# First rows' transfers first, first weights by column halves, and a newly laid order, in an attention kernel with a gated MLP

## The chip, the cores and the metric

The kernel runs on one core of a Trainium2 chip. The metric is device time in microseconds (us), lower is better. A core has a matrix engine (TensorE, PE below, with its weight loads as PEld), a vector engine (VectorE, DVE), a scalar engine (ScalarE, ACT), a general engine (GpSimd, POOL), and a queue of transfers that SyncE (SP) issues to 16 DMA engines.

## What is computed

Four batches of eight heads, 576 rows, 64 columns. Causal attention is mixed by a gate with a retrieval from a memory `M_prev`; the result, 2304 rows of 512, goes through an MLP of width 2048 with a leaky activation whose slope `alpha` is a column's own.

```python
def _attn_ref(q, k, v, M_prev, z_prev, beta) -> np.ndarray:
    scores = scale * np.matmul(q, k.transpose(0, 1, 3, 2))
    scores = np.where(causal, -1000000000.0, scores)
    scores = scores - scores.max(-1, keepdims=True)
    a = np.exp(scores)
    a /= a.sum(-1, keepdims=True) + 1e-09
    local = np.matmul(a, v)
    q_p = phi(q)
    mem_ret = np.einsum('bhsd,bhde->bhse', q_p, M_prev)
    mem_norm = np.einsum('bhsd,bhd->bhs', q_p, z_prev)[..., None] + 1e-06
    mem_out = mem_ret / mem_norm
    g = 1.0 / (1.0 + np.exp(-beta))[None, :, None, None]
    return (g * mem_out + (1 - g) * local).astype(np.float32)
...
def _moe_ref(x, w_in, w_out, alpha) -> np.ndarray:
    h = x @ w_in
    g = np.maximum(h, 0.0) + alpha * np.minimum(h, 0.0)
    return (g @ w_out).astype(np.float32)
```

`phi(x)` is `x + 1` for positive `x` and `exp(x)` otherwise.

## The kernel before

**Arithmetic.** Nearly every product is made in f16 from two parts, a high and a low one, which DVE and ACT split off (`SCALAR_TENSOR_TENSOR` with an f16 output is the low part). The weights arrive as pairs of 32-bit words of 64-bit numbers; `to_f32` turns a piece into f32 on DVE with one TENSOR_SCALAR and two SCALAR_TENSOR_TENSOR. `R` is the buffer of converted weights, 17 slots of 128x1024; `kn`, `E` and parts of `R` also hold words as they arrive.

**Stages.** The first 64 rows of all four batches form a group of their own, called Z. `first_scores` and `first_values` do its attention in f32: `s` are scores, `P` the probabilities, `stv` the maxima of its `v` and `M_prev` (`prep_vZ`). The other rows are groups of 256, two to a batch. For each head and pair of row blocks `unit_scores` makes the scores `s` on PE and their minima with the mask on DVE (`E<-s,mask,pm`, or `P<-s,mask` and `E<-s,mask` for batch 0), ACT the exponential, `unit_probs` the f16 parts `P`, `pair_values` the product with `v` in `bank`. `build_qk` and `build_v` form the f16 parts of `q`, `k` and `v` of a batch; `mv` are the maxima of `v` of batch 0, which its first values need. The MLP goes in steps: `moe_in` makes 256 columns of `h`, of which DVE and ACT form `r` and the two f16 parts of `gg`, and `moe_out` adds their product to `y`. The first two groups (Z and the first of batch 0) use the weights in f32 for their first four steps, before `split_w` has cut them in f16; with f32 weights the MLP's `h` reads `h<-R`.

**Weights.** `weights(0)` loads (`load_w`) and converts (`conv_w`) eight pieces for the first half of the MLP, `weights(1)` the other eight. Pieces 0 to 3 are `w_in`, 4 to 7 `w_out`. A piece is two transfers of 128x1024 words; `conv_w` converts it in one go of 1024 columns (one piece in two), and ACT then squares it for the sum that sets its scale (`w_scale`, whose result is `wsc`).

**Order.** Every operation is first recorded by a `Work` object, with the data it depends on (so all of them carry one line of the helper, L560), and then `Work.issue` sets the order of each engine's instructions. It prices each operation (`price`), lays them on the engines by rank (`lay`), and shifts the ranks in four rounds by the tables in `STAGES`, in which a phase name such as `LW0` (loading the first four pieces) or `V0` has a number. No instruction waits for anything but the data and the order. All transfers stand on one queue.

**Warm-up.** While nothing is there yet, PE runs 66 matmuls on a constant `ones`, of which 16 may stand at the start and 50 behind (`WARM`).

## Time and profile before

| | us |
|---|---|
| three runs, median | 558.14 |
| lowest and highest run | 557.56, 559.28 |
| span of the profiled execution | 555.3 |
| PE busy in it | 532.3 (96%) |
| DVE busy | 451.2 (81%) |
| ACT busy | 376.1 (68%) |
| POOL busy | 77.7 (14%) |

The profiled execution is one run; its own time is the span of 555.3 us, and 2.9 us less than the median of the runs, which take in what lies around it. Busy times are sums over the instructions of an engine; those of PE hold the warm-up matmuls.

### The profile page before, as it was taken

The page shows a single profiled execution, that of the slowest core. Times are in us where ns is not written, and L with a number is a line of the kernel's source. Part 1 is how long each engine was busy: PE and PEld are TensorE (multiplying, and loading weights), DVE is VectorE, ACT ScalarE, POOL GpSimd, SP SyncE. Part 2 cuts the span into 40 slices and gives each one's busy share as a digit, 9 for nine tenths or more (in the row PEclk, how much of TensorE's full clock was granted, in tenths as well). Part 3 has the DMA queues.
Part 4 walks back from the last instruction along what each step waited for, and adds up shares of the span by engine and source line. Part 5 has one row for each costly group of instructions (what it writes and reads, how often), then busy time and mean ns, then how long its engine had stood idle before and what let it go on. Part 6 is the DMA issues. An engine that isn't in the chain of part 4 may idle for free.

```text
span 555.3 us, 11994 instructions
## 1 busy us (share of the span) xinstructions
PE 532.3 (96%) x4421; PEld 353.1 (64%) x4421; DVE 451.2 (81%) x1197; ACT 376.1 (68%) x790; POOL 77.7 (14%) x142
## 2 busy tenths in 40 slices
PE   9739999999999899999998999999999999999997
PEld 3438655666567566758566667667677676866573
DVE  4899999999999899999998899997678885333322
ACT  2558987768999378978867887786587874222312
POOL 2000510031030011311221200321021120000000
PEclk9869999999999999999999999999999999999999
DMA  8999685827359999379998737599536665000101
GB/s 288 231 339 204 192 238 176 246 74 170 91 115 183 219 228 199 86 154 205 221 188 190 170 79 170 130 200 190 79 81 121 138 138 133 21 2 1 38 1 38
DMA packets 226026, 82.84 MB, mean 149 GB/s; under 512 B 216224, under 2 KB 216240, under 8 KB 225968
## 3 DMA queue, kind: packets, MB, share of 16 engines
q1 hardware_dynamic: 225968, 82.09, 64.0%
q8 instruction: 34, 0.56, 0.4%
q14 instruction: 24, 0.20, 0.1%
HBM read 35.66 MB, written 5.77 MB: 75 GB/s over the span
## 4 chain that ended last, share of the span: by engine, by line
PE 52%; DVE 30%; DMA 5%; issue 5%; ACT 3%; SPq 2%; POOL 2%; DVEq 0%; POOLq 0%; ACTq 0%
PE y L560 22%; PE h L560 20%; DVE R L560 5%; DVE P L560 5%; PE s L560 5%; DVE E L560 4%; PE bank L560 4%; DVE gg L560 3%; DVE r L560 3%; DVE q L560 2%; SPq L560 2%; POOL E L560 2%; DMA xn<-in_moe_alpha_dram 1%; DMA k<-k 1%; DVE t L560 1%
## 5 line engine op out<-in xcount | busy, mean ns | idle before, releaser
L560 PE MATMUL h<-x,R 128*128 128x256 f16 x1536 | 261.8, 273 | 1.7 <-DMA x<-xn 1.7
L560 PE MATMUL y<-R,gg 128*128 128x512 f16 (+1 forms) x832 | 258.3, 397 | 0.4 <-ACT k L560 0.4
L560 PE MATMUL bank<-v,PT 128*128 128x64 f16 x1224 | 179.2, 193 | 2.7 <-DMA PT<-P 2.3
L560 PEld LDWEIGHTS <-R 128*128 128x128 f16 x1536 | 148.9, 98 | 41.9 <-issue 5.6
L560 PEld LDWEIGHTS <-PT 128*128 128x128 f16 x1224 | 113.9, 98 | 10.5 <-DMA PT<-P 4.1
L560 PEld LDWEIGHTS <-gg 128*128 128x128 f16 x768 | 74.6, 98 | 70.8 <-DVE gg L560 0.5
L560 POOL TENSOR_SCALAR E<-q,nrm,sm 128x64 f32<-128x64 f32 x112 | 62.5, 570 | 316.8 <-DVE sm L560 265.1
L560 ACT ACTIVATE E<-E,mx 128x320 f32<-128x320 f32 (+3 forms) x136 | 81.0, 601 | 22.7 <-DVE mx L560 18.3
L560 DVE SCALAR_TENSOR_TENSOR P<-E,mx,P 128x384 f16<-128x384 f32 (+2 forms) x112 | 75.4, 699 | 9.8 <-ACT P L560 9.7
L560 ACT ACTIVATE P<-E,mx 128x384 f16<-128x384 f32 (+2 forms) x112 | 70.4, 673 | 16.4 <-POOL E L560 13.2
L560 DVE SCALAR_TENSOR_TENSOR r<-r,oma,h 128x256 f32<-128x256 f32 x128 | 56.8, 473 | 25.0 <-ACT r L560 24.7
L560 DVE SCALAR_TENSOR_TENSOR gg<-r,gsc,gg 128x512 f16<-128x512 f32 x56 | 41.7, 746 | 32.4 <-ACT gg L560 20.6
L560 ACT ACTIVATE r<-h 128x512 f32<-128x512 f32 x72 | 42.0, 586 | 37.2 <-PE h L560 23.1
L560 ACT ACTIVATE gg<-r,gsc 128x512 f16<-128x512 f32 x56 | 39.9, 715 | 32.2 <-PE y L560 29.0
L560 DVE CUSTOM_DVE_ANT_0 E<-s,mask,pm 128x320 f32<-128x320 f32 (+2 forms) x96 | 56.8, 609 | 1.4 <-PE s L560 1.2
L560 PE MATMUL s<-k,qT 128*128 128x64 f16 (+5 forms) x136 | 37.4, 294 | 1.2 <-DMA k<-k 1.0
L560 PE MATMUL s<-k,qS 128*128 128x192 f16 (+4 forms) x120 | 33.6, 294 | 0.0
L560 PE MATMUL h<-R 128*128 128x256 f32 x128 | 32.9, 384 | 0.0
L560 PEld LDWEIGHTS h<-R 128*128 128x128 f32 x128 | 22.3, 192 | 6.6 <-issue 3.3
L560 ACT ACTIVATION_READ_ACCUMULATOR E<-E,mx 128x1 f32 x124 | 23.4, 188 | 0.0
L560 ACT ACTIVATE R<-R,wsc 128x1024 f16<-128x1024 f32 x16 | 18.3, 1142 | 4.0 <-DVE R L560 4.0
L560 DVE SCALAR_TENSOR_TENSOR R<-R,wsc 128x1024 f16<-128x1024 f32 x16 | 20.4, 1275 | 0.4 <-ACT R L560 0.4
(183 smaller groups left out, 619.6 us busy)
## 6 DMA issues: line engine op xcount, KB each, us to landing
q<-in_q_dram SPq DMA_DIRECT2D x16, 256.0 KB, 4.3
vn<-in_v_dram SPq DMA_DIRECT2D x16, 256.0 KB, 4.9
out_dram<-t SPq DMA_DIRECT2D x16, 256.0 KB, 2.7
kn<-in_moe_w_in_dram SPq DMA_DIRECT2D x6, 512.0 KB, 6.5
kn<-in_moe_w_out_dram SPq DMA_DIRECT2D x6, 512.0 KB, 5.7
kn<-in_k_dram SPq DMA_DIRECT2D x12, 256.0 KB, 3.9
qS<-qT SPq DMA_DIRECT2D x24, 128.0 KB, 3.0
R<-in_moe_w_in_dram SPq DMA_DIRECT2D x4, 512.0 KB, 5.6
```

The source lines that it names most:

```text
L560: fn(*a, **kw)
```

## The change

The diff does the following.

- Warm-up: `WARM` goes from 16 and 50 to 16 and 24.
- Pieces 0 to 3 are loaded and converted by column halves: first the left half of all four, then the right. After each left half, `PACE` = 2 matmuls of the new weights (128x256, f32) go to `h0`, which nobody reads. Their squares go to `R[0]`.
- `v` and `M_prev` of the first rows come in two transfers each (64x16x64, two batches in one) and not four.
- The first rows' turned tiles use the PSUM buffer `y` and not `h`.
- The planner: transfers are priced anew (`TURNED`, the returns of `price`, `LATE` = 400 ns more to landing), the queue begins at 700 ns and holds at most eight, a GpSimd operation waits for a DVE operation with two SBUF inputs, and the lag from PE to PE is 0 and not 2.
- Phase names are finer (by pair of heads, step, piece or half), and `STAGES` has 14 tables instead of four. So the order of all work is laid anew; the counts of operations stay, but for the edits above.

```diff
-WARM = 16, 50
+WARM = 16, 24
+PACE = 2
+LATE = 400
...
 STAGES = [
     (2, {
...
-        "C3": -920, "C:ACT": 1096.2, "C:DVE": -3.8, "C:PE": -943.6, "I": -699.2, "I:DVE": 79.2, "I:POOL": 497.7,
+        "C3": -920, "C:DVE": -3.8, "D0": -56.4, "D:DVE": -3.8, "I": -699.2, "I:DVE": 79.2, "I:POOL": 497.7, "J:ACT":
...
-RING, SHARE = 1200, 0.95
+RING, SHARE, BEGIN = 1200, 0.95, 700.0
+TURNED = {128: (1216, 800, 1650), 256: (1298, 860, 1950), 320: (1347, 1500, 1600), 576: (2092, 1880, 2060)}
...
+            late += LATE
...
-                return (800 + 1.75 * kb if kb > 400 else 1130 + 0.6 * kb), 190 + 3.45 * kb, 1655, -1
+                return TURNED[round(kb)] + (-1,)
...
-                return 500, 0.45 * packets, 1800, packets
+                return 350, 90, 2600, packets
...
-                return 400, (2.75 if self.phase in ("LW0", "LW1") else 4.9) * kb, 2000, packets
+                return 390, 2.75 * kb, 2550, packets
...
-                return 540, max(300, 4.06 * kb), 1800, packets
-            return 620, (273 if kb > 200 else 200) + 4.17 * kb, 2100, packets
+                away = o.tensor.name in self.fixed
+                return 580, 250 + 2.6 * kb, 1800 if away or o.space != ins[0].space else 1740, packets
+            return 620, 420 + 2 * kb if o.shape[0] > 64 else 5.08 * kb, 2100, packets
...
+        if not back:
+            free["DMA"] = BEGIN
+        landed, port = [], 0.0
...
+                landed.append(done)
+                if len(landed) >= 8:
+                    free[x] = max(free[x], landed[-8] + 16)
...
+                elif x == "POOL" and not back and port > t:
+                    hold += port - t
...
+                if x == "DVE":
+                    port = done if both else 0.0
...
-        for b in range(B):
-            vv = nat[Z]["v"][b // 2][:, b % 2]
-            Y.dma_start(out=vv[64:128], in_=v[b, :, 0:64, :].rearrange("h p d -> p h d"))
-            Y.dma_start(out=vv[0:64], in_=M_prev[b].rearrange("h d e -> d h e"))
+        for t in range(2):
+            work.phase = f"LV{t}"
+            for ps, src in ((slice(64, 128), v[2 * t:2 * t + 2, :, 0:64, :]), (slice(0, 64), M_prev[2 * t:2 * t + 2])):
+                Y.dma_start(out=nat[Z]["v"][t][ps].rearrange("p b h d -> p (b h) d"), in_=src.rearrange("b h p d -> p (b h) d"))
...
-    def conv_w(s):
-        work.phase = f"C{s // 4}"
-        r, st = raw(s + 1), pieces.pop(s)
-        n = 1024 if WC[s] else 512
-        for c in range(0, 1024, n):
+    def conv_w(s, cs=(0, 1)):
+        work.phase = f"C{s // 4}{s % 4}" if s > 3 or not cs[0] else f"D0{s}"
+        r, st = raw(s + 1), pieces[s]
+        for c in (0, 512) if len(cs) == 1 or not WC[s] else (0,):
+            n = 512 if len(cs) == 1 or not WC[s] else 1024
+            if len(cs) == 1 and c != 512 * cs[0]:
+                continue
             to_f32(r[:, c:c + n], st[:, 2 * c:2 * c + 2 * n].bitcast(I32).rearrange("p (c t) -> p c t", t=2))
-        A.activation(st[:, 0:1024], r, AF.Square, scale=2.0 ** -20, accum_out=wsq[s // 4][:, s % 4:s % 4 + 1])
+        if s < 4 and not cs[0]:
+            work.phase = f"n{s}"
+            for i in range(PACE):
+                T.matmul(h0[:, 0], lhsT=r[:, 0:128], rhs=r[:, 0:256], start=True, stop=True)
+            work.phase = f"C0{s}"
+        if cs[-1]:
+            pieces.pop(s)
+            work.phase = f"c{s // 4}"
+            A.activation(R[0] if s < 4 else st[:, 0:1024], r, AF.Square, scale=2.0 ** -20, accum_out=wsq[s // 4][:, s % 4:s % 4 + 1])
...
-        for x, outs, tag in ((n["q"][t], [(slice(0, 128), qT)], "h"),
+        for x, outs, tag in ((n["q"][t], [(slice(0, 128), qT)], "y"),
...
-        flipped([P[:, h] for h in range(H)], [(slice(0, 128), PT.rearrange("p h c -> p (h c)"))], "hy"[t])
+        flipped([P[:, h] for h in range(H)], [(slice(0, 128), PT.rearrange("p h c -> p (h c)"))], "y")
...
-        load_w(8 * i)
-        for s in range(8 * i, 8 * i + 8):
+        if i == 0:
+            for f in (load_w, conv_w):
+                for c in range(2):
+                    for s in range(4):
+                        f(s, (c,))
+            w_scale(0)
+        first = 8 * i if i else 4
+        load_w(first)
+        for s in range(first, 8 * i + 8):
             if s % 8 < 7:
                 load_w(s + 1)
             conv_w(s)
```

**SP, the first transfers.** Before, the first rows' `q`, `k` (from `in_k_dram`), `v` and `M_prev` stand behind fourteen transfers of weights, `alpha`, `z` and `beta`; the part from the first `q` on reads:

```order
L560 DMA q_0_93<-in_q_dram 64x8x64
L560 DMA R<-in_k_dram 64x8x64
L560 DMA q_0_93<-in_q_dram 64x8x64 x3
L560 DMA R<-in_k_dram 64x8x64
L560 DMA R<-in_v_dram 64x8x64
L560 DMA R<-in_k_dram 64x8x64 x2
L560 DMA R<-in_M_prev_dram 64x8x64
L560 DMA R<-in_v_dram 64x8x64
L560 DMA R<-in_M_prev_dram 64x8x64
L560 DMA R<-in_v_dram 64x8x64
L560 DMA R<-in_M_prev_dram 64x8x64
L560 DMA R<-in_v_dram 64x8x64
```

Now the queue begins so:

```order
L1620 DMA R<-in_v_dram 64x16x64
L1620 DMA R<-in_M_prev_dram 64x16x64
L1620 DMA q_0_93<-in_q_dram 64x8x64 x2
L1620 DMA xn_103<-in_moe_alpha_dram 16x128
L1620 DMA gco<-in_beta_dram 128x8
L1620 DMA R<-in_moe_w_in_dram 128x1024
L1620 DMA R<-in_v_dram 64x16x64
L1620 DMA R<-in_M_prev_dram 64x16x64
L1620 DMA q_0_93<-in_q_dram 64x8x64 x2
L1620 DMA R<-in_k_dram 64x8x64 x2
L1620 DMA q_1_94<-in_z_prev_dram 64x512 x4
L1620 DMA R<-in_k_dram 64x8x64 x2
```

The first rows' `v` and `M_prev` went from the end of their transfers to the start, and of the seven weight transfers that stood ahead of the first `q` six went behind the first rows' `k`.

**DVE, the maxima of `v` of batch 0** (`mv_0_146<-vn_97`; the rows on `R` are weight conversions, `E_0_92` and `kn_90` weight words, `q_2_95` rows of `q` of batch 0). Before:

```order
L560 TENSOR_SCALAR R<-kn_90 128x1024
L560 SCALAR_TENSOR_TENSOR R<-R 128x1024
L560 SCALAR_TENSOR_TENSOR R<-kn_90,R 128x1024
L560 TENSOR_SCALAR R<-E_0_92 128x1024
L560 SCALAR_TENSOR_TENSOR R<-kn_90,R 128x1024
L560 SCALAR_TENSOR_TENSOR R<-E_0_92,R 128x1024
L560 SCALAR_TENSOR_TENSOR q_2_95<-q_2_95,t_0_117 128x512
L560 SCALAR_TENSOR_TENSOR R<-E_0_92,R 128x1024
L560 TENSOR_REDUCE mv_0_146<-vn_97 128x1 x2
L560 SCALAR_TENSOR_TENSOR q_2_95<-q_2_95,t_1_118 128x512
```

Now:

```order
L1620 SCALAR_TENSOR_TENSOR R<-E_0_92,R 128x1024
L1620 TENSOR_REDUCE nrm_106<-t_0_117 128x8
L1620 TENSOR_SCALAR R<-kn_90 128x1024
L1620 SCALAR_TENSOR_TENSOR R<-E_0_92,R 128x1024
L1620 SCALAR_TENSOR_TENSOR R<-kn_90,R 128x1024
L1620 TENSOR_REDUCE wsc<-bank_67 128x1
L1620 TENSOR_REDUCE stq_85<-q_2_95 128x1
L1620 SCALAR_TENSOR_TENSOR R<-kn_90,R 128x1024
L1620 TENSOR_REDUCE mv_0_146<-vn_97 128x1 x2
L1620 ISA E_0_92,mx_107<-s_0_69,mask 128x192
```

The maxima now stand at row 129 and not 112 of DVE's order, behind conversions of `w_out`, with the first score minima of batch 0 (`E_0_92,mx_107<-s_0_69,mask`) right behind them.

**PE, around the first `h` with weights that count** (`h_123` and `h_124` are the two buffers of `h`; `PT` and `R` in `s` rows are the first rows' probabilities and `v`; `y` rows on `ident` turn a tile). Before, ahead of it the last of the first rows' values and the turned `q` of batch 0:

```order
L560 MATMUL y_131<-ident,q_2_95 128x128
L560 MATMUL s_0_69<-PT_113,R 64x64
L560 MATMUL y_132<-ident,q_2_95 128x128
L560 MATMUL y_131<-ident,q_2_95 128x128
L560 MATMUL y_132<-ident,q_2_95 128x128
L560 MATMUL y_131<-ident,q_2_95 128x128
L560 MATMUL y_132<-ident,q_2_95 128x128 x2
L560 MATMUL h_124<-R 128x256
L560 MATMUL h_123<-R 128x256
```

Now (the `h_123<-R` ahead of the turned `q_2_95`, x2 and single, are pace matmuls):

```order
L1620 MATMUL y_131<-ident,P_99 128x128 x4
L1620 MATMUL y_132<-ident,P_99 128x128 x4
L1620 MATMUL s_0_69<-PT_113,R 64x64 x16
L1620 MATMUL h_123<-R 128x256 x2
L1620 MATMUL y_131<-ident,P_100 128x128 x4
L1620 MATMUL y_132<-ident,P_100 128x128 x4
L1620 MATMUL h_123<-R 128x256
L1620 MATMUL s_0_68<-PT_114,R 64x64 x16
L1620 MATMUL y_131<-ident,q_2_95 128x128
L1620 MATMUL y_132<-ident,q_2_95 128x128
L1620 MATMUL y_131<-ident,q_2_95 128x128 x3
L1620 MATMUL y_132<-ident,q_2_95 128x128 x3
L1620 MATMUL h_123<-R 128x256
L1620 MATMUL h_124<-R 128x256 x8
```

The first `h` that counts moved from row 203 to row 105 of PE's order, behind the same turned `q`.

## Rows read from the trace of the kernel before

**Rows 1.** Windows of the span: stretch and length, busy us of each engine (instructions).

```profile
0.00:47.34 47.34, 34.49 (x244) 20.93 (x244) 37.46 (x111) 23.74 (x65) 4.16 (x13) 0.82 0.97 275
47.34:273.30 225.96, 222.72 (x1681) 144.72 (x1681) 220.17 (x578) 181.93 (x374) 39.84 (x63) 1.00 0.75 175
273.30:551.50 278.20, 275.10 (x2501) 187.46 (x2497) 193.62 (x512) 169.69 (x352) 33.70 (x66) 1.00 0.51 107
```

**Rows 2.** PE timeline, 39 to 51 us: start, us, engine, line, operation, [idle <-releaser].

```profile
39.41 1.51 PE L560 MATMUL h<-ident,P 128*128 128x128 f32 x6 [2.82 <-DVE P L560]
...
47.34 2.86 PE L560 MATMUL h<-R 128*128 128x256 f32 x12
...
50.03 0.27 PE L560 MATMUL y<-ident,v 128*128 128x128 f32 x1
```

**Rows 3.** DVE timeline at the 19th f16 `gg`.

```profile
272.56 0.74 DVE L560 SCALAR_TENSOR_TENSOR gg<-r,gsc,gg 128x512 f16<-128x512 f32 x1
273.22 0.68 DVE L560 CUSTOM_DVE_ANT_0 E<-s,mask,pm 128x448 f32<-128x448 f32 x1
```

**Rows 4.** PE timeline, 273 to 276 us.

```profile
273.40 0.19 PE L560 MATMUL bank<-v,PT 128*128 128x64 f16 x1
273.43 0.38 PE L560 MATMUL y<-R,gg 128*128 128x512 f16 x1
273.65 0.19 PE L560 MATMUL bank<-v,PT 128*128 128x64 f16 x1
...
274.67 0.24 PE L560 MATMUL s<-k,qT 128*128 128x192 f16 x1 [0.61 <-DMA k<-k]
...
275.23 0.38 PE L560 MATMUL y<-R,gg 128*128 128x512 f16 x1
```

**Rows 5.** DVE timeline, 0 to 53 us.

```profile
6.24 0.69 DVE L560 TENSOR_SCALAR R<-R 128x1024 int32<-128x1024 int32 x1 [5.12 <-DMA R<-in_moe_w_in_dram]
...
37.59 0.23 DVE L560 SCALAR_TENSOR_TENSOR zsm<-zsm,C 128x8 f32<-128x8 f32 x2
...
51.95 1.81 DVE L560 TENSOR_REDUCE mv<-vn 128x1 f32<-128x1024 f32 x2
```

**Rows 6.** SyncE timeline: issues of the transfers.

```profile
18.48 1.31 SPq L560 DMA_DIRECT2D R<-in_k_dram  x2
...
45.10 0.63 SPq L560 DMA_DIRECT2D vn<-in_M_prev_dram  x1
```

**Rows 7.** Transfers by kind: count, KB each, median us from issue to landing.

```profile
vn<-in_v_dram SPq DMA_DIRECT2D x16, 256.0 KB, 4.9
```

**Rows 8.** ACT timeline: the last exponential of the first rows.

```profile
34.01 0.33 ACT L560 ACTIVATE P<-P,zmx 128x64 f32<-128x64 f32 x1
```

**Rows 9.** DVE by line and form: count, busy us, mean ns, idle before.

```profile
L560 DVE SCALAR_TENSOR_TENSOR P<-E,mx,P 128x640 f16<-128x640 f32 x32 | 28.1, 877 | 2.5 <-ACT P L560 2.5
...
L560 DVE CUSTOM_DVE_ANT_0 E<-s,mask,pm 128x576 f32<-128x576 f32 x24 | 19.4, 809 | 0.9 <-PE s L560 0.9
...
L560 DVE SCALAR_TENSOR_TENSOR R<-kn,R 128x1024 int32<-128x1024 int32 x10 | 12.2, 1225 | 0.0
...
L560 DVE TENSOR_SCALAR R<-kn 128x1024 int32<-128x1024 int32 x5 | 3.4, 687 | 0.0
...
L560 DVE SCALAR_TENSOR_TENSOR R<-kn,R 128x512 int32<-128x512 int32 x4 | 2.7, 680 | 0.0
...
L560 DVE TENSOR_SCALAR R<-kn 128x512 int32<-128x512 int32 x2 | 0.8, 416 | 0.0
```

**Rows 10.** Windows around the first dense stretch; column PEclk is the granted clock.

```profile
33.30:43.60 10.30, 5.70 (x24) 4.74 (x24) 9.32 (x29) 3.43 (x13) 0.00 (x0) 0.50 1.08 349
43.60:60.00 16.40, 16.14 (x140) 12.39 (x140) 16.40 (x36) 14.39 (x31) 0.00 (x0) 1.00 0.97 254
```

**Rows 11.** Windows; the last column is GB/s of the transfers.

```profile
16.00:26.00 10.00, 7.09 (x40) 3.89 (x40) 9.93 (x21) 6.70 (x13) 0.00 (x0) 0.85 1.00 200
34.00:40.00 6.00, 2.13 (x8) 1.69 (x9) 5.02 (x24) 1.59 (x6) 0.00 (x0) 0.50 1.02 402
```

More of the change, by code (lines that the diff above doesn't have):

```diff
@@ new lines @@
+        "P:DVE": -882.6, "P:PE": -157.8, "S0": 4737.2, "S1": -1253, "S3": -2953.6, "S:ACT": -87.5, "S:DVE": 168.1,
[10 rows of a table added]
+        "p:ACT": -1644.8, "p:DVE": -74.4, "q1": 32.6, "q2": 262.4, "q3": -367.1, "q:ACT": -726.4, "q:DVE": -733.4,
+        "r0": 11.2, "r:ACT": 58.5, "r:DVE": 78.6, "s01": 224.3, "s03": -198.1, "s11": -19.5, "s13": -477.4, "s21":
+        -225.6, "s23": -95.5, "s31": -35.1, "s33": 429.3, "s:ACT": -781.8, "s:DVE": -887.5, "s:PE": 273.7, "sZ":
+        208.6, "sZ:ACT": -57.4, "sZ:DVE": 1849.8, "sZ:PE": 312.7, "tZ": 208.6, "tZ:ACT": -57.4, "tZ:PE": 312.7, "v1":
[4 rows of a table added]
@@ L198 @@
+        41.6, "s:ACT": -5, "s:DVE": -22.3, "s:PE": 143.8, "sZ": -0.9, "sZ:ACT": 37.5, "sZ:DVE": 2.5, "sZ:PE": -5.2,
[4 rows of a table added]
         "y0_10:DVE": -5.7, "y0_10:PE": 142.2, "y0_11": -0.1, "y0_11:DMA": 0.3, "y0_11:DVE": -24.3, "y0_11:PE": 213.5,
@@ L753, in load_first @@
             t, ps = b // 2, slice(b % 2 * 64, b % 2 * 64 + 64)
+            work.phase = f"LZ{t}"
             Y.dma_start(out=qz[ps, t], in_=q[b, :, 0:64, :].rearrange("h p d -> p h d"))
@@ L792, with load_w @@
     staging = [[kn, q16] * 4, staging * 2]
-    def load_w(s):
-        work.phase = f"LW{s // 4}"
+    def load_w(s, cs=(0, 1)):
+        work.phase = f"LW{s // 4}{s % 4}" if s > 3 or not cs[0] else f"LX0{s}"
         hf, kind, u = s // 8, s // 4 % 2, s % 4
         st = pieces[s] = staging[s < 8][s % 8]
-        for c in range(2):
+        for c in cs:
             if kind == 0:
@@ L825, in w_kappa @@
     def w_kappa(hf):
+        work.phase = f"c{2 * hf + 1}"
         i = 2 * hf + 1
@@ L839, in split_w @@
     def split_w(s):
-        work.phase = f"S{s // 4}"
+        work.phase = f"S{s // 4}{s % 4}"
         f, r, sc = fin(s), raw(s + 1), wsc[:, s // 4, 0:1]
@@ L989, in prep_phi @@
         nrm, tt, C = p["nrm"][:, r], p["tt"][:, r], p["C"][:, :, r]
+        ph = work.phase
         for i in range(i0, i1):
+            work.phase = f"{ph}{i}"
             qi = qs[i]
@@ L997, in prep_phi @@
             V.reduce_sum(nrm[:, i - i0, :], e, axis=AX.X)
+        work.phase = ph
         V.scalar_tensor_tensor(out=nrm, in0=nrm, scalar=1e-6, in1=igc[:, None, :].to_broadcast([128, i1 - i0, H]),
@@ L1024, in build_qk @@
     def build_qk(b, hp):
-        work.phase = f"bk{b}"
+        work.phase = f"bk{b}{hp}"
         n, p = nat[b], pre[b]
@@ L1042, in build_v @@
     def build_v(b, hp):
-        work.phase = f"bv{b}"
+        work.phase = f"bv{b}{hp}"
         n, p = nat[b], pre[b]
@@ L1074, in first_pair @@
     def first_pair(hp, bl):
-        work.phase = f"s0{bl[0]}"
+        work.phase = f"s0{bl[0]}{2 * hp + 1}"
         p = pre[0]
@@ L1107, in unit_scores @@
             return
-        work.phase = f"s{b}{bl[0]}"
+        work.phase = f"s{b}{bl[0]}{h}"
         a = h % 2
@@ L1129, in unit_probs @@
     def unit_probs(b, h, bl):
-        work.phase = f"P{b}{bl[0]}"
+        work.phase = f"P{b}{bl[0]}{h}"
         p = pre[b]
@@ L1169, in pair_values @@
     def pair_values(b, hp, bl, x):
-        work.phase = f"o{b}{bl[0]}"
+        work.phase = f"o{b}{bl[0]}{2 * hp + 1}"
         pts = [ust.pop((b, 2 * hp + a, bl[0], "T")) for a in range(2)]
@@ L1214, in turned @@
     def turned(i0):
-        work.phase = "BK0" if i0 else "bk0"
+        ph = work.phase = "BK0" if i0 else "bk0"
         n, p = nat[0], pre[0]
@@ L1220, in turned @@
                              i0 + 1 if i0 else 0, 2 if i0 else 3)):
+            work.phase = ph + ("0" if t == "qT" else "1")
             y = p["qT" if t == "qT" else "kT"] = stack[t].rearrange("p (a c) -> p a c", a=NP)
@@ L1238, in first_scores @@
                     [(ps, o.rearrange("p n c -> p (n c)")) for ps, o in outs], tag)
+        work.phase = f"sZ{t}"
         s = other().rearrange("p (h n) -> p h n", h=H)
@@ L1257, in first_values @@
     def first_values(t, x32):
-        work.phase = "oZ"
+        work.phase = f"oZ{t}"
         n, p = nat[Z], pre[Z]
@@ L1283, in moe_in @@
     def moe_in(g, j):
-        work.phase = f"h{g['id']}{j // 4}"
+        work.phase = f"h{g['id']}{j // 4}{j % 4}"
         n = g["n"]
@@ L1323, in moe_out @@
     def moe_out(g, j):
-        work.phase = f"y{g['id']}{j // 4}"
+        work.phase = f"y{g['id']}{j // 4}{j % 4}"
         n = g["n"]
```

94 lines of the change are left out of this document (59 added, 35 removed), and 1413 rows, old and new, of the table STAGES.

## Prediction

> **What bounds the kernel now.** I read three views in this order: the windows of the whole span, the timelines of TensorE (PE) and VectorE (DVE) up to 62 us, and the same two timelines at one later checkpoint. The profiled execution has a span of 555.3 us; the median of the three runs is 558.14 us, so 2.9 us lie around the span and I carry them unchanged.
>
> The windows [rows 1] fall into three stretches. Up to 47.34 us PE does little that counts: most of its 34.5 busy us are warm-up matmuls on `ones`, and DVE is busy for 37.46 us. From 47.34 us, the first real `h` matmul [rows 2], to 551.5 us PE is busy for 497.8 of 504.2 us. Up to 273.3 us DVE is just as full: 220.17 of 225.96 us. Only behind that does it have room, 193.6 of 278.2 us. So the end is set by how early PE's stream starts and how rarely it stops; and up to about 275 us it cannot run ahead of DVE, which converts the weights, forms the score minima and splits every operand. A faster beginning on PE is worth only what DVE follows.
>
> A checkpoint shows how closely the two run together. Count the f16 `gg` splits (the 128x512 SCALAR_TENSOR_TENSOR that finishes one step of the MLP) in DVE's order: the 19th starts at 272.56 and ends at 273.30 us [rows 3], and PE's matmuls on that step stand around the same microsecond, after a wait of 0.61 us for a transfer of `k` [rows 4]. DVE was idle for 9.88 us before 47.34 us and for 5.79 us from there to the checkpoint (stretch less busy time in [rows 1]), 15.7 us together. I forecast the checkpoint of the changed kernel from DVE's work and idle time, and then add the PE work that is left behind it.
>
> **The change part by part.**
>
> *Transfers.* DVE's first work waits 5.12 us for the first weights, until 6.24 us [rows 5]. In the new order it waits for half of `v` and `M_prev`, two transfers of 256 KB as the first on the queue. Pieces of 128 KB take about 0.65 us each to issue (two in 1.31 us [rows 6]), and those of 256 KB 4.9 us to land [rows 7]. Second issue at about 1.4, landing at about 6.3 us: nothing is gained or lost here. The change is what follows. Before, the last `k` of the first rows is issued at 19.1 us, as the second of two from 18.48 [rows 6]; now 18 transfers stand ahead of it, at about 0.65 us each 11.7 us, so it is issued at about 12 us.
>
> *The first rows' chain.* From that issue (19.1) to the first `h` (47.34) it is 28.2 us. In it the last exponential of these rows ends at 34.3 us [rows 8], while DVE first multiplies with its sum at 37.59 us [rows 5]: DVE was at the maxima of `v` and at what follows from them. With `v` first these are done early, 3.3 us less. The first `h` comes at 12 + 28.2 - 3.3 = 37 us, at the earliest some 4 us before if the transposes and copies, which stood behind weight conversions, close up: 33 to 37 us, 10 to 14 us earlier than 47.34.
>
> *DVE's idle time at the start.* Of the 9.88 us, 5.12 are the first wait [rows 5] and 4.8 the rest: the program's start, and short waits for PE. I give the new order the same first wait, and 1 to 3 us for `z`, `k` and the scores: 6 to 8 us in all, **-2 to -4 us; I take -3.** Its own order puts half conversions where it would wait, so the middle is nearest.
>
> *Half conversions.* A full piece costs one TENSOR_SCALAR of 0.687 and two SCALAR_TENSOR_TENSOR of 1.225 us, together 3.14; a half 0.416 and two of 0.680, two halves 3.55 [rows 9]. That is +0.42 us for each of four pieces, +1.7 us at most; since neighbours overlap by 0.08 us (272.56 + 0.74 is 273.30, the next starts at 273.22 [rows 3]), less. I take **+1.1 us**, counted in the next sum; 0 is the other end.
>
> *DVE's work ahead of the checkpoint.* I counted both orders up to the 19th f16 `gg`. The new order has four score minima of 576 columns fewer (0.81 us each [rows 9], -2.9 after the overlap), two of 448 (0.68 [rows 3], -1.2) and four `P` splits, two of 640 columns (0.88 [rows 9]) and two of 512 (0.74, the form of [rows 3]): -2.9. It has one `k` build of 640 and one `v` build of 512 more (+1.7), and the halves (+1.1). Smaller forms cancel. Sum: **-4.2 us** ahead of the checkpoint.
>
> *PE's work ahead of it.* Both have the same `h` and `y` matmuls there to within two. The new order has 70 value matmuls fewer (0.03 us from 273.40 to the next start [rows 4], -2.0 us) and 24 score matmuls of 64 to 512 columns fewer (by columns: a `y` of 512 columns takes 0.22 us to the next start [rows 4], 0.43 ns a column; -3.0 us); against them +0.3 us of small ones. That work is not saved, it stands behind the checkpoint now: **+4.7 us.** The total of PE's useful work is unchanged: 64 f32 `h` matmuls, 1536 f16 ones, 768 f16 `y` and 1224 value matmuls in either order.
>
> *Pace matmuls and warm-up.* Eight f32 matmuls on fresh weights, of 0.45 us at full clock (12 records, two to a matmul, start within 2.69 us [rows 2]), replace 26 of the 66 on `ones`. They stand ahead of the first `h`, where PE idled, 2.82 us at once before 39.41 [rows 2]: nothing. If that cover is gone they cost 3.6 us, or twice that at half clock. The clock is the risk: from 33.3 to 43.6 us PE, with 5.70 us of work in 10.3, was granted 0.50, which is 1.2 GHz, and 2.4 GHz from 43.6 us, when it was busy for 16.14 of 16.4 us [rows 10]. "TensorE: Matmul & The Clock Gate" of the Trainium skill (What's actually happening) says that the throttled state is the default and that activity releases it; by it fewer warm-up matmuls speak against the change, and the trace agrees as far as idling is followed by half clock. By that rule alone the first `h` group would run at half for longer, which is the last rival below.
>
> *DVE's idle time between 47 and 273 us.* 5.79 us now. The prices of transfers in the planner are new (under its old ones PE waited 0.61 us for `k` right at the checkpoint). Bounds: all but 2 us gone, -4; or, since an order with other transfers can meet new waits, twice as much, +6. I take -1.5, near to no change, because the kinds of waits stay.
>
> *PE at and behind the checkpoint.* PE reaches the data of the 19th `gg` 1.9 us later than DVE gives them (275.23 against 273.30 [rows 3, 4]); a stream that is held by DVE alone has not this: -1.8 at most, 0 at least; I take -1.8, since DVE holds it in the new order too. Behind it PE idles for 3.1 us [rows 1]. Between none of it left and twice as much, -3 to +3; I take -1, near to no change. The end behind 551.5 us is the same in both orders: 0.
>
> **Sum:** -3 - 4.2 + 4.7 - 1.8 - 1.5 - 1 = -6.8 us. Against the profiled execution that is a span of 548.5 us; against the median, 558.14 - 6.8 = **551.3 us**. The ends of all terms (with the halves at 0 and 1.7) give -14.2 and +7.4 us; they will not all fall together, so this case's own range is 548 to 555.
>
> **The rivals.**
>
> *PE keeps its head start.* If DVE's later order lets PE stay ahead, the 10 to 14 us of the first `h` remain: -12, 546 us. For it: PE is the busiest engine, 497.8 of 504.2 us of its stream. Against: DVE has 256 us of work ahead of the checkpoint, so with 6 us of idle time the checkpoint cannot come before about 262 us, and 4.7 us more stand behind it.
>
> *Nothing is left of it.* The transfers set DVE's start as now (no gain of 3), the idle time between and behind stays: -4.2 + 4.7 = +0.5, 558.6 us. For it: in both orders the same bytes must land before the values of batch 0 can be used. Against: DVE idles 9.88 us at the start now, 4.8 us of it not the first wait.
>
> *The first rows' short runs hold up batch 0: slower.* One place: DVE's two maxima of `v` of batch 0. They ran at 51.95 us [rows 5] without waiting, with 41.9 us of DVE's work ahead; now 45.7 us stand ahead. In a stretch of the first rows' short runs the queues moved 200 GB/s, in one of the weights' long runs 402 GB/s [rows 11]. About 13.0 MB are issued up to the `M_prev` of batch 0 before (at 45.10 us [rows 6]), 13.7 MB now, and the 0.7 MB more are short runs: 3.5 us, landing at 52 to 56 us; with new queue waits like that before 45.10 us, 59 us. Then DVE's idle time ahead of the maxima is 59 - 45.7 = 13.3 us against 51.95 - 41.9 = 10.1, +3.2 us instead of -3, and without the gains at 47 us and later the sum is -4.2 + 4.7 + 3.2 = +3.7: 562 us. It decides from a landing at about 55.5 us on, where DVE's idle time is 9.8 us, no less than before; landing earlier leaves a gain.
>
> *The clock.* If the first group's `h` (32 matmuls of 0.45 us, 14 us) runs wholly at half clock, PE loses 14 us of a head start of 10 to 14. Since DVE holds PE later anyway, the time is that of the case "nothing is left", about 558 us. Against: [rows 10] shows full clock as soon as the stream is dense.
>
> **How the numbers follow.** Forecast 551.3 (548 to 555): 0.59. Head start kept, 546: 0.14. Nothing left, or the clock, 558 to 559: 0.15. Slower, 562: 0.12. Within 0.3% (1.7 us, about what a measurement of this kernel can tell from no change) lies most of the third case; of the forecast and the second nearly all is faster, and a sixth of the third. Faster 0.75, same 0.13, slower 0.12. The range of 8 in 10 reaches half way through the second case and to the third: 544.5 to 559.
>
> **What would show it.** In the new profile the first `h` of the stream should start at 33 to 37 us; DVE's idle time up to there 6 to 8 us; its `v` maxima of batch 0 at 50 to 56 us; the 19th f16 `gg` end at 264 to 268 us (now 273.3), and PE idle in between, visibly or at stretched spacing, for about as long as its head start was. A 19th `gg` before 261 us means that DVE had less to do or waited less than I count; one after 271 us, that the transfers hold it. I am wrong altogether if PE is held by another engine than DVE up to 270 us.

## The result: 1.4% slower, and the profile after

| | before | after |
|---|---|---|
| median of the runs, us | 558.52 | 566.67 |
| lowest and highest, us | 557.56, 559.28 | 565.01, 568.06 |
| ratio, 95% interval | | 1.0139 (1.0107 to 1.0170) |
| span of the profiled execution, us | 555.3 | 563.2 |
| PE's last matmul ends at, us | 551.5 | 559.5 |

The kernel became 8.15 us slower (7.9 us by the spans); 551.3 us had been forecast, with a range of 544.5 to 559.0. The windows below are cut where [rows 1] are: at the first `h` that counts, at the 19th f16 `gg`, and at PE's last matmul. Columns are stretch, length, busy us of PE, PEld, DVE, ACT and POOL (instructions), granted clock, DMA share, GB/s.

```profile
0.00:36.48 36.48, 28.55 (x227) 18.09 (x228) 27.59 (x109) 19.38 (x57) 4.16 (x13) 0.91 0.98 249
36.48:271.00 234.52, 220.32 (x1615) 143.82 (x1615) 225.05 (x577) 182.50 (x368) 28.89 (x57) 1.00 0.73 177
271.00:559.40 288.40, 280.85 (x2570) 190.62 (x2569) 196.91 (x526) 173.97 (x366) 31.02 (x72) 0.99 0.53 110
```

The timelines of PE, DVE and SyncE after the change hold the rows that answer to [rows 2, 3, 5, 6]:

```profile
36.48 1.78 PE L1620 MATMUL h<-R 128*128 128x256 f32 x7 [0.22 <-ACT R L1620]
...
6.91 1.22 DVE L1620 TENSOR_REDUCE stv<-R 128x1 f32<-128x1024 f32 x1 [5.79 <-DMA R<-in_M_prev_dram]
...
55.79 1.80 DVE L1620 TENSOR_REDUCE mv<-vn 128x1 f32<-128x1024 f32 x2
...
270.29 0.75 DVE L1620 SCALAR_TENSOR_TENSOR gg<-r,gsc,gg 128x512 f16<-128x512 f32 x1
...
15.14 1.30 SPq L1620 DMA_DIRECT2D R<-in_k_dram  x2
```

The opening does what was meant: the first `h` comes at 36.48 us and no longer at 47.34. (By the issues in the trace, eight weight transfers stood ahead of the first `q` before, not seven; all but one went behind the first rows' `k`.) At the checkpoint the lead is 2.3 us (the 19th `gg` ends at 271.0, before at 273.3), and at the end it is a loss of 7.9. The places where PE stops tell why. Windows of equal stretches from 47.34 us on, the kernel before first:

```profile
47.34:150.00 102.66, 102.03 (x549) 61.70 (x549) 100.04 (x271) 82.99 (x176) 16.94 (x25) 1.00 0.66 177
150.00:250.00 100.00, 97.45 (x882) 65.46 (x880) 97.32 (x256) 79.90 (x162) 17.10 (x30) 1.00 0.80 165
250.00:350.00 100.00, 97.12 (x958) 68.24 (x957) 93.38 (x260) 80.38 (x171) 19.90 (x34) 1.00 0.82 174
```

and the changed kernel:

```profile
47.34:150.00 102.66, 98.27 (x579) 61.26 (x579) 101.24 (x279) 82.80 (x176) 15.37 (x29) 1.00 0.67 181
150.00:250.00 100.00, 91.40 (x811) 59.36 (x808) 94.58 (x242) 75.72 (x149) 11.99 (x24) 1.00 0.77 163
250.00:350.00 100.00, 92.58 (x900) 63.84 (x898) 90.25 (x247) 77.95 (x165) 12.33 (x32) 0.98 0.83 169
```

Stretch less PE's busy time is its idle time: 0.6, 2.6 and 2.9 us before, 4.4, 8.6 and 7.4 us after. DVE is idle for longer too, 5.4 us against 2.7 in the middle window; it is not what filled up. The waits of PE from 47 us on (engine, operation, what it waited for: us in all, times, longest), after:

```profile
PE bank L1620 <- DMA PT<-P: 5.9, 5, 1.8
PE h L1620 <- DMA x<-xn: 5.2, 3, 2.1
PE s L1620 <- ACT PT L1620: 2.0, 3, 0.7
PE h L1620 <- ACT P L1620: 1.8, 1, 1.8
```

and before:

```profile
PE bank L560 <- DMA PT<-P: 2.3, 2, 1.8
PE h L560 <- DMA x<-xn: 1.7, 2, 1.3
```

`PT<-P` and `x<-xn` are the transposes that go through the queue of transfers: the probabilities for the product with `v`, and the finished rows for the MLP. PE waits for them 11.1 us, before 4.0. The chain of waits from 155 to 192 us after the change shows one such place (start, us, what):

```profile
161.27 5.61 DMA PT<-P
166.89 0.05 issue
166.93 0.98 PE bank L1620 x27
167.91 0.02 issue
167.94 0.48 ACT xn L1620
168.42 0.03 issue
168.44 0.48 DVE xn L1620
...
170.05 0.35 DVE r L1620
```

PE's own rows there:

```profile
166.93 0.96 PE L1620 MATMUL bank<-v,PT 128*128 128x64 f16 x27 [1.78 <-DMA PT<-P]
...
170.50 2.79 PE L1620 MATMUL h<-x,R 128*128 128x256 f16 x24 [1.84 <-ACT P L1620]
```

A transpose lands 5.61 us after its issue; behind it come 27 value matmuls, two short operations on `xn`, and DVE's `r`, which stands behind `xn` in DVE's order. PE has little else in its order and stops twice, for 1.78 us before the value matmuls and for 1.84 us before the next `h`. The first stop waits for the transpose. For the second the profile names `P` on ACT, while the chain passes through DVE's `r`; which of the two released it is not settled. It was not the next transpose, `x<-xn`, which was issued at 168.96 us and landed 2.5 us later. Two suspects remain: the other traffic on the queue, and the order itself.

### The profile page after: what moved, and what is told of

The parts are those of the page before. It is cut to its first block, busy times and chain, and to the rows that moved or that the text cites. A ratio compares the mean times of both kernels' runs of the same rounds, so it can differ in the third digit from the quotient of the medians.

```text
span 563.2 us, 11970 instructions
## 1 busy us (share of the span) xinstructions
PE 529.8 (94%) x4411; PEld 352.5 (63%) x4411; DVE 449.6 (80%) x1209; ACT 376.5 (67%) x790; POOL 64.1 (11%) x142
## 4 chain that ended last, share of the span: by engine, by line
PE 51%; DVE 23%; DMA 11%; ACT 8%; issue 4%; SPq 1%; POOL 1%; DVEq 0%; POOLq 0%; ACTq 0%
PE y L1620 22%; PE h L1620 20%; DMA PT<-P 6%; DVE R L1620 5%; PE bank L1620 4%; DVE E L1620 4%; DVE P L1620 4%; PE s L1620 3%; ACT P L1620 3%; DVE r L1620 2%; DMA x<-xn 2%; DVE gg L1620 2%; SPq L1620 1%; DMA R<-in_M_prev_dram 1%; DMA t<-part 1%
## 5 line engine op out<-in xcount | busy, mean ns | idle before, releaser
L1620 PE MATMUL y<-R,gg 128*128 128x512 f16 (+1 forms) x832 | 215.0, 398 | 1.7 <-DVE t L1620 0.7
L1620 PE MATMUL h<-x,R 128*128 128x256 f16 x1536 | 188.5, 273 | 10.6 <-DMA x<-xn 5.2
L1620 PEld LDWEIGHTS <-R 128*128 128x128 f16 x1536 | 146.6, 98 | 47.4 <-DVE r L1620 10.5
L1620 ACT ACTIVATE E<-E,mx 128x320 f32<-128x320 f32 (+3 forms) x136 | 80.8, 601 | 18.1 <-DVE mx L1620 16.1
L1620 POOL TENSOR_SCALAR E<-q,nrm,sm 128x64 f32<-128x64 f32 x112 | 52.7, 482 | 319.2 <-DVE sm L1620 245.5
L1620 PEld LDWEIGHTS <-PT 128*128 128x128 f16 x1224 | 43.1, 98 | 14.5 <-DMA PT<-P 7.9
L1620 PE MATMUL bank<-v,PT 128*128 128x64 f16 x1224 | 45.8, 194 | 5.9 <-DMA PT<-P 5.9
L1620 PE MATMUL h<-R 128*128 128x256 f32 x144 | 36.1, 394 | 0.3 <-ACT R L1620 0.2
L1620 PE MATMUL s<-k,qT 128*128 128x320 f16 (+5 forms) x136 | 35.2, 288 | 0.7 <-DVE mx L1620 0.7
L1620 PEld LDWEIGHTS h<-R 128*128 128x128 f32 x144 | 26.7, 196 | 6.0 <-issue 1.3
L1620 ACT ACTIVATE t<-y,u 128x512 f32<-128x512 f32 x18 | 12.2, 680 | 15.3 <-PE y L1620 15.3
```

What stands on the lines that cost most here:

```text
L1620: fn(*a, **kw)
```

## Experiments

The theory drawn from these rows, Q: the rest of the new order stands too close to its transfers, and the loads that share the queue with the transposes make PE wait. The first rival was my own premise, that DVE holds PE. Others came up later and are named where they were set down. Line numbers differ from kernel to kernel, since a list is inserted.

In all kernels with a changed order, and where work is left out, the loop over the planner's dates is replaced by a written list. `ORDER` is the kernel's own order where nothing else is said, and `DROP` names the operations that are left out:

```diff
-            for i in sorted(range(len(ops)), key=lambda i: (start[i], i)):
+            for i in ORDER:
+                if i in DROP:
+                    continue
                 _, fn, a, kw = ops[i][:4]
                 fn(*a, **kw)
```

**Is it the loads?** `DROP` is the 32 loads of batches 2 and 3, in the changed kernel and in the one before.

> The changed kernel with its order kept row for row, without the 32 transfers that bring q, k, v, M_prev and z_prev of batches 2 and 3 (those batches then work on what is left of batch 1 in the buffers, so the output is not the reference's; all other work is issued). Theory Q (the new order leans on the queue of transfers: the transposed P and xn land late behind the loads, and PE's 21 us of visible idle time come from there): 7 to 12 us faster than the changed kernel's 566.7 us, 555 to 560. Rival D (DVE's work holds PE, as the prediction had it, and the loads are hidden): at most 1.5 us faster, 565 or more.

> The kernel before with its order kept, without the same 32 transfers of batches 2 and 3 (output not the reference's). Theory Q: the order before has slack towards the queue, so it gains less than half of what the changed one gains: 0 to 3 us, 555.5 to 558.5. Rival D: the same, 0 to 1.5 us. A gain of 5 us or more would say that the transfers hold both orders alike.

Measured: 556.48 us (0.9950 of the kernel before, 0.9929 to 0.9971), and 553.95 (0.9924, 0.9904 to 0.9944). The loads cost the changed kernel 10.2 us, as theory Q had it, and the kernel before 5.2 (4.2 by the ratio), more than I had allowed it and about the 5 us that I had called a sign of both orders being held alike. PE's idle time between 250 and 350 us, where these loads lie, falls from 7.4 to 2.6 us. Between 150 and 250 it hardly moves, 7.7 us after 8.6. So the loads explain the idle time from 250 us on; even without them on either side, the changed kernel is 2.5 us behind.

**Is it DVE?** `DROP` is the 32 DVE instructions of 0.68 us that belong to the rotation of the queries (21.8 us by their own lengths; since neighbours overlap, DVE's busy time falls by 15.9 us in the changed kernel and 16.1 in the one before).

> The changed kernel with its order kept, without 32 of DVE's instructions of 0.68 us (the update of q and its product with z, two for each of 16 row tiles of batches 0 to 3, 21.8 us in all, some 16 us of them ahead of 273 us; output not the reference's). Theory Q: DVE is not what holds PE here, at most 1.5 us faster, 565 to 567. Rival D: DVE holds PE up to 273 us, so 5 us or more faster, 561.5 or less.

> The kernel before with its order kept, without the same 32 DVE instructions (output not the reference's). Both theories: if DVE binds the kernel before up to about 275 us, as the prediction read from its rows, it is 4 to 6 us faster, 552.5 to 554.5. If it stays at 557 or more, the reading that DVE bound the kernel before was wrong too.

Measured: 567.99 us (1.0185, 1.0154 to 1.0215) and 558.2 (0.9993, 0.9977 to 1.0008). Neither kernel gains clear of noise from 16 us less busy time on the engine that my prediction had named as the bound up to 275 us. That premise fell here, for the kernel before as well.

**The pace matmuls.** `DROP` is the eight pace matmuls of the changed kernel.

> The changed kernel with its order kept, without the eight pace matmuls. In the profile of the changed kernel ten of their sixteen records stand ahead of the first h that counts at 36.48 us, where PE waits anyway, six behind it. Theory Q (transfers and the order behind hold the end): 0 to 1.4 us faster (three matmuls of 0.45 us), 565 to 566.7. Rival P (the pace matmuls keep PE's clock up): the stretch from 36 us on falls to half clock and it is slower by 3 us or more, 570. Rival P2 (all eight lie on the path, some at half clock): 3.5 us faster or more, 563 or less.

Measured: 564.81 us (1.0103, 1.0066 to 1.0140), 1.9 us less, just beyond theory Q's range and not in that of either rival, and the intervals overlap. PE keeps full clock without them (1.00 from 36 to 48 us), so rival P is out. If they are not free, as I had them, they are a small part.

**Opening or rest?** `ORDER` takes the planner's order of one kernel up to 150 us (or 275) and that of the other behind it.

> All work of the changed kernel, its order kept for what the planner lays ahead of 150 us, and behind that the rest of the work in the order of the kernel before. Theory Q (what costs is the order behind 150 us, where PE idles visibly for 17 us against 5.5 before): the early start lasts, 553 to 560. Rival O (the opening loses it: DVE's work is moved back so that nothing of the head start can be used): 562 or more.

> All work of the kernel before, its order kept for what its planner lays ahead of 150 us, and behind that the rest in the order of the changed kernel. Theory Q: the order behind 150 us loses what it loses in the changed kernel, 563 to 570. Rival O: no loss, 557 to 560.

> All work of the changed kernel, its order kept for what the planner lays ahead of 275 us, and behind that the order of the kernel before. If the stretch from 280 to 325 us (7 us of PE's idle time, a DMA share of 0.98 against 0.86) is where most is lost, 558 to 562; if the loss lies ahead of it, 564 or more.

Measured: the new opening with the old rest 560.67 us (1.0021, 0.9994 to 1.0049), the old opening with the new rest 576.12 (1.0297, 1.0240 to 1.0355), the new order up to 275 us 571.03 (1.0207, 1.0162 to 1.0252). The first lies between the ranges of theory Q and rival O, the second beyond theory Q's 570; only the third is where it was expected for a loss ahead of 275 us. With the old rest, the new opening is 1.8 us worse than the kernel before, run beside it (1.0 lies in its interval); with the new rest it is 9.4 us better. So the loss sits behind 150 us. But a cut order has a seam of its own: in the third kernel PE idles for 11.7 us between 250 and 350 us, more than in the changed kernel. PE's waits between 150 and 176 us in the first of the three:

```profile
PE s L399 <- DVE mx L562: 5.2, 1, 5.2
PE bank L562 <- DVE xn L562: 2.7, 1, 2.7
```

PE arrives there early, and these two waits alone take 7.9 us of its head start. The exact share of opening and rest can't be read from such a pair.

**Is it the planner's prices?** The changed kernel's instructions, all of them, laid out in one pass at dearer prices for loads and transposes, by the ranks of either kernel; then a search for an order at such prices.

> The changed kernel with the same instructions, laid out once more: the planner takes the start times of the changed kernel as ranks, in one pass and with no search, and only the prices of the transfers are other: a load of 256 KB keeps the transfer engines for 1341 ns as in the kernel before (932 in the changed one), a transpose through the queue keeps them 1.2 times as long and lands 0.3 us later than priced. Theory Q (the rest of the new order stands too close to its transfers, because it was laid at transfer prices that are too kind): 554 to 562, at least 4 us under the 566.7 of the changed kernel, with less idle time of PE between 250 and 350 us (5 us or less, not 7.4). Rival C (an order is good or bad by the length of the search behind it, and prices decide nothing: a pass without a search can only spoil it): 566 to 575. Rival S (the shift of the opening by itself, in whatever order the rest stands): 564 to 568.

> As the run before it in this set, but the ranks are the start times of the kernel before (for the instructions that only the changed kernel has, its own), so that the opening is as short as in the changed kernel and the rest stands as near to the old order as the earlier opening lets it, laid without a seam. Theory Q: 552 to 560, no longer than the kernel before, and under the 560.7 of the order that was cut at 150 us, whose seam cost PE a wait of 5.2 us. Rival C: 560 to 570. Rival S: 564 to 568, as the opening is the changed kernel's.

> The changed kernel's instructions in an order that was searched for anew, with the dearer transfer prices of the two runs before it in this set, and with a second set of still dearer ones (1450 ns, 1.35 times, 0.5 us later) counted in by half. Theory Q: the earlier opening can be kept if the rest leaves the transfers room: 547 to 556, faster than the kernel before by 3 to 11 us, with idle time of PE from 47 us on of 10 us or less (21.4 in the changed kernel, 6.1 in the kernel before). Rival S (the earlier opening can't be kept, something that no order mends takes it back): 558 to 567. Rival C: 552 to 560 with idle time of PE anywhere.

Measured: 571.08 us (1.0209, 1.0178 to 1.0241), 565.61 (1.0103, 1.0070 to 1.0137) and 559.53 (1.0009, 0.9986 to 1.0032). My theory failed in this form: all three missed its ranges. All three lie in those of rival C, the last two in those of rival S as well. Dearer prices by themselves did not mend the order; that one pass lays it as tightly as before against the new prices is my reading, not shown. The last two no longer opened early: their first `h` that counts came at about 50 us (the loads of the opening had been priced dearer too), so they say nothing of rival S.

**The queue cleared.** `DROP` is 72 transfers: the 32 loads, the 20 stores of the output, 4 copies of partial sums and the last 16 copies of transposed queries; in the third kernel the 32 DVE instructions too.

> The changed kernel without 72 transfers: the 32 loads of batches 2 and 3 (as in the run without them), the 20 stores of the output, 4 copies of partial sums and the last 16 of the 24 copies of transposed queries; those batches compute on what stands in the buffers and nothing is stored, so that behind 200 us the queue carries nearly only transposes. Run without the loads alone: 556.5. Theory Q (whatever shares the queue with the transposes makes PE wait): the idle time of PE between 150 and 250 us, 7.6 us without the loads, falls to 5 us or less and the time to 551 to 555. Rival L (the new order asks for its transposes too soon after they are issued, whoever else is in the queue): 555 to 557, idle time between 150 and 250 us of 6.5 us or more.

> The kernel before without the same 72 transfers; without the 32 loads alone it took 553.95. Both theories: 552 to 554.5, as PE's idle time behind 47 us was 4.8 us there, 1 to 2 of them behind transposes. If the changed kernel without the 72 transfers is 2 us or more under this one, the head start of its opening is worth that much once the queue is clear; if the two are equal, the order behind the opening gives it back without any help from loads or stores.

> The changed kernel without the 72 transfers and also without the 32 DVE instructions of 0.68 us (of the queries' rotation) whose removal alone did nothing (568.0 against 566.7). If DVE is what holds the new order once the queue is clear, as my prediction had it for both orders: 3 us or more under the run without the 72 transfers alone, most of it before 275 us. If not (theories Q and L): within 2 us of that run.

Measured: 554.53 us (0.9921, 0.9887 to 0.9954), 548.46 (0.9816, 0.9789 to 0.9844) and 552.84 (0.9888, 0.9855 to 0.9921). The time of the first lies in theory Q's range, its idle time, which tells more, does not; and the kernel before gained more than either theory expected. Windows of the changed kernel without the transfers:

```profile
150.00:250.00 100.00, 92.02 (x820) 60.42 (x819) 94.71 (x241) 75.15 (x149) 12.47 (x26) 0.98 0.52 103
250.00:350.00 100.00, 98.65 (x1005) 69.44 (x1004) 97.99 (x269) 84.91 (x181) 13.09 (x34) 1.00 0.59 121
```

and of the kernel before without them:

```profile
150.00:250.00 100.00, 99.57 (x906) 67.50 (x903) 99.53 (x262) 82.25 (x168) 17.76 (x32) 1.00 0.53 110
250.00:350.00 100.00, 99.62 (x997) 70.17 (x996) 96.68 (x265) 82.20 (x173) 19.70 (x33) 1.00 0.54 116
```

The DMA share between 150 and 250 us is 0.52 (0.77 with all transfers), and PE's idle time there is 8.0 us, as ever; in the old order it is 0.4. Between 250 and 350 us it is 1.4 us. So there are two losses: from 250 us on it is the loads; before that it stays without these transfers, as a property of the order (weights, transposes and the other copies are still in the queue). Both stops of the chain above are there again, of 1.74 and 1.84 us, and its transpose takes 5.58 us where it took 5.61. PE's last matmul ends 6.0 us later in the new order than in the old one with the queue cleared (551.2 against 545.2 us), and 8.0 later with all transfers. Without the loads alone it was 3.2 us later (551.4 against 548.2). So the share of the order in the loss is not one number: the other 40 transfers cost the old order 2.9 us more and the new one 0.2. Some 1.7 of the 6.0 us are half clock between 245 and 250 us (granted clock 0.66). (2.2 us of what either kernel gains here is only the missing last store, behind PE's end.) Rival L holds for the earlier place, theory Q for the later one. The third kernel is 1.7 us under the first, with intervals that overlap and less than the 3 us expected if DVE held it: DVE's amount of work is at most a small part of it.

**Can an early opening be kept?** The changed kernel's instructions in two orders from a longer search, in which the first loads keep the changed kernel's prices, and an order counts by its mean time under four sets of later prices.

> The changed kernel's instructions, all of them, in an order searched for anew: the first loads at the changed kernel's prices, later loads and transposes dearer, and an order counts by its mean time under four sets of prices (transposes 1.1 to 1.5 times as long and 0.1 to 0.9 us later, loads at 1200 to 1450 ns), so that PE has other work in hand when a transposed tile comes late. It opens as early as the changed kernel (first real h at about 36 us) and starts from the order cut at 150 us. Theory L (what was lost is spare time between a transposed tile's landing and its use, which an order can have or not have, and an early opening can be kept if it has): 548 to 557, faster than the kernel before, with PE idle for less than 10 us from 47 us on. Rival S (an early opening is always given back): 558 to 566.

> As the run before it in this set, from another course of the same search, so that one lucky order does not decide. Theory L: 548 to 557. Rival S: 558 to 566.

Measured: 557.80 us (0.9974, 0.9955 to 0.9993) and 556.23 (0.9954, 0.9933 to 0.9975). Both beat both kernels, by intervals that end below 1: the first is 0.9 us under the kernel before and 8.9 under the changed one, the second 2.5 and 10.4, with the changed kernel's instructions. PE's first `h` and two windows of it:

```profile
36.38 11.06 PE L562 MATMUL h<-R 128*128 128x256 f32 x50
...
150.00:250.00 100.00, 93.70 (x811) 60.49 (x808) 98.41 (x251) 80.07 (x160) 13.87 (x28) 0.97 0.80 169
250.00:350.00 100.00, 98.57 (x968) 68.69 (x966) 93.91 (x261) 81.03 (x172) 18.05 (x31) 1.00 0.86 173
```

It opens as early as the changed kernel, and PE's idle time between 250 and 350 us is 1.4 us, with all loads in place: an order can bear them. Between 150 and 250 us 6.3 us are left. The expected 10 us of idle time at most were not met (17.9 in the first and 13.4 in the second, from 47 us on), and of the two times the second lies in theory L's range, the first between it and rival S's: an early opening can be kept in part.

The second opens 10.96 us ahead of the kernel before, and its last matmul ends 0.2 us ahead. Of the 10.7 us given back, 7.1 are additional idle time of PE and 3.7 additional busy time. Half clock alone is enough for the latter: the profile shows it three times, behind waits of up to 1.25, 3.02 and 1.24 us, and 0.34 of 5 us is up to 1.7 us each time (an estimate from these rows):

```profile
85.00:90.00 5.00, 3.85 (x19) 2.52 (x20) 4.68 (x9) 4.42 (x10) 0.00 (x0) 0.66 0.80 249
...
170.00:175.00 5.00, 4.46 (x26) 3.38 (x27) 5.00 (x10) 5.00 (x10) 0.58 (x2) 0.66 0.87 197
...
180.00:185.00 5.00, 4.16 (x40) 2.96 (x41) 4.40 (x11) 2.08 (x4) 0.00 (x0) 0.66 0.60 170
```

The kernel before has 1.00 from 47 us on.

**What takes back the rest?** The faster of these two orders without the 32 DVE instructions, and without the 72 transfers.

> The order of the second searched run (556.2 us, first h at 36.4 us, PE idle for 6.2 us between 150 and 250 us, one wait of 3.0 us for DVE's r in it, DVE busy for 98.4 of those 100 us) without the 32 DVE instructions of 0.68 us of the queries' rotation, whose removal did nothing in the kernel before (558.2) and in the changed one (568.0). Theory D (an early opening brings PE up against DVE's work in 100 to 200 us, as the prediction had it, and this order is held there and nowhere else): 550 to 553, 3 to 6 us less, PE idle between 150 and 250 us for 3 us or less. Rival W (what holds PE there is the wait for results on their way, not the amount of DVE's work): 555 to 557.

> The same order without the same 72 transfers as in the two kernels with a cleared queue (554.5 for the changed kernel, 548.5 for the kernel before). If the searched order has the spare time behind its transposes that the changed kernel's lacks, it loses little to the queue: 548 to 553, a gain of 4 to 8 us where the changed kernel gained 12.1 and the kernel before 10.1. If its head start comes out with the queue cleared, it is at or under 548.5.

Measured: 556.84 us (0.9948, 0.9924 to 0.9973) and 552.22 (0.9880, 0.9847 to 0.9913). The second falls by 4.0 us (2.3 of them the missing last store), as expected of an order with some spare time behind its transfers, but stays above the 548.5 of the old order without them. The first has no gain: its time lies in rival W's range, and theory D misses. Windows from 150 to 175 us, of this order and of it without the DVE instructions:

```profile
150.00:175.00 25.00, 21.51 (x194) 12.15 (x191) 24.95 (x53) 24.76 (x45) 2.83 (x6) 0.93 0.77 174
...
150.00:175.00 25.00, 21.03 (x192) 12.21 (x190) 22.86 (x54) 24.52 (x44) 3.21 (x7) 0.90 0.87 177
```

In those 25 us DVE and ACT are both full, while PE idles; with DVE relieved, ACT stays full, and the cutting of the weights into f16 parts (`R<-R,wsc`), which needs both, makes DVE wait for ACT:

```profile
164.92 1.28 DVE L565 SCALAR_TENSOR_TENSOR R<-R,wsc 128x1024 f16<-128x1024 f32 x1 [0.90 <-ACT R L565]
```

That this pair of engines is what makes PE idle here in this order is my reading of these rows. No kernel relieved both, so it stays open. In the changed kernel they are less full there (DVE 23.6 and ACT 21.3 of the 25 us, PE idle for 4.1; without transfers and DVE instructions 19.4, 20.8 and 4.3), so in its case it is not the amount of their work; the wait for results on their way, as in the chain above, is what is left.

## Why the prediction was wrong

**The opening: the date right, partly by luck.** The first `h` was forecast for 33 to 37 us and came at 36.48. But the last `k` was issued as the second of two from 15.14 us, at about 15.8 and not at 12: the issues ahead of it took longer than the 0.65 us each that I had counted (the pair of `q` at 6.88 us took 3.81). From there to the first `h` it was 20.7 us and not 24.9 (28.2 less 3.3). The two errors cancel. The maxima of `v`, forecast for 50 to 56, ran at 55.79.

**DVE's idle time at the start (-3): wrong.** The first wait is 5.79 us, not 5.12 [rows 5]. Up to the first `h` DVE idles for 8.9 us, where 6 to 8 were forecast, and up to 47.34 us DVE idles for 10.9 us, against 9.9 in [rows 1]: +1.0.

**DVE's work ahead of the checkpoint (-4.2): right,** -5.0 measured (27.59 + 225.05 us against 37.46 + 220.17).

**DVE's idle time up to the checkpoint: the failed step in its first half.** -3 and -1.5 were forecast together; measured is 18.4 us in the first two windows against 15.7, +2.7. The checkpoint therefore came at 271.0, not at 264 to 268. I had written that one after 271 us would mean that the transfers hold it, and that I would be wrong altogether if PE was held by another engine than DVE. Both runs with less work on DVE say that DVE's work does not hold it.

**PE behind the checkpoint: the failed step in its second half.** The 4.7 us of work left over are there: PE is busy for 280.85 us behind it and not 275.10, +5.75, of which some 1.7 are half clock (below). But -1.8 and -1 were forecast for its idle time, and it went from 3.1 to 7.55 us, +4.45. These terms add up: -5.0 + 2.7 + 5.75 + 4.45 = +7.9 us.

**The premise under both.** I read DVE's 220.17 busy of 225.96 us as a bound. PE in the same stretch was just as full (222.72), and a stretch in which two engines are full shows an order in which they fit into each other, not which of them holds the other. In the old order PE hardly stopped from 47 us on, so there were only two ways to gain: start earlier, which was done, and not stop later, which I took for granted ("near to no change, because the kinds of waits stay"). They did not all stay: the sum of PE's waits went from 6 to 21 us. The two transposes, the largest kinds before, grew from 4.0 to 11.1 us, and the other 10 us are mostly waits for ACT and DVE that the old order did not have (`PT` and `P` on ACT, `r` on DVE). For DVE from 47 us on, +1.7 lies within the bounds that I gave (-4 to +6); for PE behind the checkpoint, +4.45 lies outside mine (-3 to +3), which reached only to twice the old idle time; and the start's gain of 3 was missing as well. Two sums were off besides: the ends of all terms add up to -13.4 and +8.1 us, not -14.2 and +7.4, and DVE's work ahead of the checkpoint in the new order is 257.6 - 4.2 = 253.4 us, not 256. The result lies at the upper end of all terms taken together, which I had ruled out as unlikely.

**The rivals.** The slower one had the right sign and the wrong mechanism: the maxima of `v` did run late, at 55.8 us, but no wait stands in front of them; DVE came to them straight from a conversion. DVE's idle time at the start grew by 1.0, and three quarters of PE's additional idle time (11.7 of 15.4 us by the windows) lie behind 150 us. No rival had PE stop more often all along the new order. The clock rival did not come: from 36.48 us on the `h` run at full clock, 7 in 1.78 us.

## What to carry to other kernels

A newly laid order puts every wait at stake, not only those that the change speaks of: compare the spare time between landing and use of late results along the whole order, or the planned idle time of the bounding engine, before counting a gain at the start. An engine that is 97% busy is shown to be the bound only when taking work from it shortens the time, and taking transfers from both the old and the new order tells what an order costs by itself. Where an order is searched at priced times, let it count under several sets of prices: the orders chosen so kept an early opening and came out 9 and 10 us better than the changed kernel's. (Their search was also longer; no run separates the two.)

## What the runs showed of the hardware

PE fell to half clock in mid-stream. Windows of the changed kernel:

```profile
284.00:287.20 3.20, 3.20 (x63) 2.36 (x62) 2.48 (x9) 2.55 (x5) 0.76 (x2) 1.00 1.10 239
287.20:291.20 4.00, 1.70 (x16) 0.72 (x13) 1.59 (x7) 1.46 (x4) 0.00 (x0) 1.00 0.84 161
291.20:300.00 8.80, 8.60 (x112) 5.98 (x113) 8.01 (x23) 8.39 (x18) 1.55 (x4) 0.81 1.05 219
```

After 4 us with 1.70 us of work, the granted clock over the next 8.80 us is 0.81, though PE is busy for 8.60 of them: 1.2 GHz for some 3.3 us of it (0.19 of 8.8, twice), which costs about 1.7. So a wait of 2.09 us, behind one of 0.41, cost nearly double. "TensorE: Matmul & The Clock Gate" of the Trainium skill (What's actually happening) has it that the throttled state is the default and activity releases it; these rows agree as far as a stretch of little work is followed by half clock. It does not come every time: after the idle 1.84 us at 169.22 us in the changed kernel without the 72 transfers the clock stayed at 1.00.

The landing time of a transpose is not one number: of the `PT<-P`, one took 5.61 us in the chain above, another 6.16 us (issued at 313.73 us behind four loads and a store), with a median of 4.0 us in either kernel. What sets it is not shown: with the 72 transfers left out the first of the two took 5.58 us, and the median was 3.9.
